# Top-k attention and a feed-forward block: the first pair of rows in two groups, weight shifts spread over four steps, and the second block's statistics one step earlier

## The chip, the cores and the metric

The kernel runs on one core of a Trainium2 chip. A core has five engines that each work through their own list of instructions in order: TensorE (PE in the profile; its weight loads are listed as PEld), VectorE (DVE), ScalarE (ACT), GpSimd (POOL) and SyncE (SP), which here only issues DMAs. An engine that needs another's result waits on a semaphore. The metric is the device time of one execution in microseconds, as the median of several runs.

## The reference

Two parts follow each other. The first is attention that keeps, for every query, the 32 largest scores; the second is layer normalisation, a feed-forward pair of matrices and a residual. All is float32, except that `w_ch1` and `w_ch2` are given as float64.

```python
# q, k, v: (8 batches, 8 heads, 576 rows, 64)
scores = scale * q @ k^T                                  # 576 x 576 for each batch and head
kth = np.partition(scores, -32)[..., -32:-31]
scores = np.where(scores >= kth, scores, -1e9)
attn = exp(scores - max); attn = attn / (sum(attn) + 1e-9)
x = (attn @ v)  as (8, 576, 512)                          # heads side by side
xn = (x - mean) / sqrt(var + 1e-6) * g_ln                 # over 512
out = x + max(xn @ w_ch1, 0) @ w_ch2                      # 512 -> 2048 -> 512
```

## The kernel before, in words

**Units, jobs, groups.** Queries are taken 128 rows at a time: four tiles of 128 and a rest of 64 per batch. A *job* is one batch, two heads side by side (`hp` from 0 to 3) and a list of such row tiles; a *unit* is one row tile of a job, for both heads. There are 160 units, and the first eight (`EARLY`) are the row tiles 0 and 1 of batch 0 for the four pairs of heads. Each job has one *group* (`Group`): its units share one transposed tile `pt`, one product with the values and one set of denominators. `pt` has a single buffer.

**Steps.** The loop `for n in range(END)` (L1266) writes out one step per unit. In step n, VectorE selects for unit n while the other engines work for its neighbours; every engine gets its instructions in the order in which this loop writes them, and nothing is reordered later. What a step does, by engine:

- PE: the scores of unit n+2 (`scores`, L434), the transposes of the weights of an earlier unit (`turn`, L602), the product with the values when a group is complete (`values`, L665 and L673) and its transposes (`place`, L710). Between these, `fill` (L269) puts pieces of the feed-forward blocks, which wait in the list `todo`.
- ACT: copies the scores from PSUM (`take_scores`, L415), scales the thresholds (`prepare`, L491 and L492), makes the mask (`mask`, L528), the exponentials (`weigh`, L539), and copies what PE transposed (L614, L642, L683). `put` (L687) scales a result into `x`.
- DVE: eight rounds on 288 columns. At the end of step n-1, `halve` splits unit n into the larger and the smaller of each two columns (L457 maximum, L458 minimum). Then `select(u, 0)` to `select(u, 3)`: MAX8 (L479, L471) finds eight largest, MATCH_REPLACE8 (L465) takes them out. `select(u, 3)` stands at the end of the step.
- POOL: subtracts the scores from the mask (L531) and writes a check (`watch`, L498).

**Weights.** The float64 weights are turned into float32 on the chip, in 32 *pieces* of 128 x 512 (class `Piece`): 0 to 15 of `w_ch1`, 16 to 31 of `w_ch2`. `fetch` (L148, SP) loads both 32-bit words; `split` has ACT take the high word's size (L164) and the low word (L166), and POOL clamp the size (L165) and the sign (L169); `shift` (L172, DVE) joins size and sign; `join` (L178, POOL) adds the low word's part and marks the piece ready. Which piece is treated in which step stands in `batches`, and in which place of the step in `weights(n, phase)` (L205): phase 0 near the step's start, phase 1 after `select(u, 1)`, phase 2 just ahead of `select(u, 3)`, phase 3 after `halve`. Pieces 0 to 3 (`batches[-1]`) are fetched and split ahead of step 0; their four shifts stand at the end of step 0 after `halve`, and their joins one in each of the steps 0 to 3. Steps 1 to 8 take one piece each (split in phase 0, shifted in phase 2, joined in phase 3 of the next step). From step `LATE` = 9 on there are two pieces a step (fetched in phase 0, split in phase 2, shifted and joined in phase 1 of the next step), the last two in step 18.

**Blocks.** Two row tiles of 128 rows are one feed-forward block. When the last pair of heads has been placed, `arrived` notes the rows, and `Block.stats` (L738 statistics, L739 their sum) makes mean and variance and takes the mean off: in the first block on DVE (L741), in all others on POOL (L744, L747). `Block.centred` says when the transposes of the rows may follow: at once in the first block, otherwise six calls of `fill` later (`CENTRE_AGE`). The block's own work is then `turn_x` (L776, L782), the hidden layer (L822, relu L845), the projection (L861 in the first two blocks, L982 in the others), the scaling (L797) and the residual (L790). Hidden and projecting matmuls wait until their piece of the weights is ready. `gives` holds the step at which a block joins `todo`: the first block, of units 0 to 7, in step 9 (`gives_first`), the second in step 19. The first block's last group is `quick`: its product, its placing and its reciprocal (L1290) stand at the very start of step 9, and its statistics in the middle of that step. The second block's rows are placed in step 18 and its statistics stand late in step 19, after `select(u, 2)`.

**Start.** `load(fresh[0], nc.sync, nc.scalar)` brings k and q of the first job with four DMAs each, k on SP's queue and q on ACT's (L303), in runs of 32 floats; DVE transposes them (L362) into `kT`, `qT` (256 columns) and `late_qT` (320 columns). Then SP fetches pieces 0 to 3 and loads the next job, for which the first job's input tile must be free.

Of the kernel before, what the change touches and what calls it, by code (L numbers as in the profile page):

```python
# [29 lines left out]
def compute(  # L30
# [162 lines left out]
        nc.scalar.copy(gcol[:], ps[:, 0:NC])  # L193


    LATE = NF // 2 + 1
    batches = {}
    queue = list(pieces)
    for n in range(-1, NF + 4):
        count = 4 if n < 0 else 0 if n == 0 else 1 if n < LATE else 2  # L200
        batches[n], queue = queue[:count], queue[count:]
    batches = {n: x for n, x in batches.items() if x}
    assert not queue
# [1 line left out]
    def weights(n, phase):  # L205

        now, before = batches.get(n, []), batches.get(n - 1, [])
        if phase == 0:
            coming = batches.get(n + 1, [])
            for x in (coming if 0 <= n < LATE - 1 else now if n >= LATE else []):  # L210
                x.fetch()
            for x in now if 0 < n < LATE else []:
                x.split()
        elif phase == 1:
            for x in before if n > LATE else []:
                x.shift()
                x.join()
        elif phase == 2:
            for x in now if n >= LATE else []:
                x.split()  # L220
            for x in now if 0 < n < LATE else []:
                x.shift()
        else:
            for x in before if 0 < n <= LATE else []:
                x.join()

    todo = []
# [63 lines left out]
    def load(job, first, second, later=False):  # L291

        job.ins = {}
        raw = ldpool.tile([P, 2, S], FP32, tag="raw", name="kqin")
        if job.whole:
            load_rows(job, raw, first, second)
            return
        for s, (name, src, queue) in enumerate((("k", k, first), ("q", q, second))):
            t = raw[:, s]

            def part(i, t=t, src=src, queue=queue):
                head, d0 = 2 * job.hp + i * 32 // D, i * 32 % D
                queue.dma_start(  # L303
                    t[i * 32 : (i + 1) * 32, :].rearrange("b (n a) -> b n a", a=32),
                    src[job.b, head, :, d0 : d0 + 32].rearrange("(n b) a -> b n a", b=32),
                )

            for i in range(P // 32):
                if later:
                    age = (4 * len(job.ins) + i) // 2  # L310
                    loads.add(lambda i=i, part=part: part(i), -age)
                else:
                    part(i)
            job.ins[name] = t
# [407 lines left out]
    class Block:  # L722
# [9 lines left out]
        def stats(self, i):  # L732
            x = self.x[i]
            if self.mv is None:
                self.mv = small.tile([P, 2, 2], FP32, tag="mv", name="mv")
                self.rstd = small.tile([P, 2], FP32, tag="rstd", name="rstd")
            st = brief_small.tile([P, 6], FP32, tag="st", name="st")
            nc.vector.bn_stats(out=st[:], in_=x)  # L738
            nc.vector.bn_aggr(out=self.mv[:, i, :], in_=st[:])  # L739
            if now[0] <= gives_first:  # L740
                nc.vector.tensor_scalar_sub(x, x, self.mv[:, i, 0:1])  # L741
            else:
                less = brief_small.tile([P, 1], FP32, tag="less", name="less")
                nc.gpsimd.tensor_scalar(  # L744
                    less[:], self.mv[:, i, 0:1], -1.0, 0.0, ALU.mult, ALU.add
                )
                nc.gpsimd.tensor_scalar(x, x, 1.0, less[:], ALU.mult, ALU.add)  # L747
            self.step[i] = tick[0]

        def centred(self, i):  # L750
            return i in self.step and (
                now[0] <= gives_first or tick[0] - self.step[i] >= CENTRE_AGE
            )

        def inverse(self):
# [324 lines left out]
    order += [(6, rows[0] + rest), (7, rows[0] + rest), (6, rows[1]), (7, rows[1])]  # L1080
    assert B == 8
    jobs = [Job(b, hp, [qts]) for b, qts in order for hp in range(NHP)]
    units = []
    for j in jobs:
        j.groups = [Group(j, qts) for qts in j.groups]
# [29 lines left out]

    for j, after_j in zip(jobs, jobs[1:] + [None]):
        waits = after_j is not None and units[after_j.first].moved
        j.groups[0].lag = 2 if j.last < EARLY else 4 if waits else 3

    full = slice(0, P)  # L1120
    gives = {}
# [9 lines left out]
    for j in jobs:  # L1131
        if j.hp == NHP - 1:
# [3 lines left out]
            dsts = [[(out[b, t[1] * P : (t[1] + 1) * P, :], full)] for t in tiles]  # L1136
            if jobs.index(j) == NHP - 1:
                step -= 1
                j.groups[0].quick = True
            if tiles:  # L1140
                add_block(step, tiles, dsts)
            if J in j.groups[0].qts and b % 4 == 3:
# [103 lines left out]
        blk.x[i] = x  # L1246
        rows_of.setdefault(n + 1, []).append((blk, i))

    gives_first = min(gives)
    load(fresh[0], nc.sync, nc.scalar)  # L1250

    nc.scalar.copy(gcol[:], half[:])
# [13 lines left out]
    for n in range(END):  # L1266
# [89 lines left out]
            scores(units[2])  # L1356
            take_scores(units[2])
        for x in (u if n < EARLY else None, mk if n > EARLY else None):
            if x and x is units[x.job.last]:
                load_values(x.job)  # L1360
                ends_due[n + 1] = x.job
        fill()
# [33 lines left out]
            select(u, 3)  # L1396
        if nxt:
            halve(nxt)
        if n == 0:
            for x in batches[-1]:  # L1400
                x.shift()
        weights(n, 3)
        for x in batches[-1][n : n + 1]:
            x.join()
        if g and not quick and g.job.hp == NHP - 1:
            for qt in g.qts:
                if qt < J:
                    arrived(n, (g.job.b, qt), xs[g.job.b, qt])
        if late and late.job.hp == NHP - 1:
            r = late.job.b // 2  # L1410
            if r % 2:
# [61 lines left out]
```

## Time and profile before

| | us |
|---|---|
| median of 3 runs | 1550.89 (1550.7 to 1552.42) |
| the profiled execution | 1550.43 |
| its span | 1548.6 |
| PE busy in the span | 1463.6 (95%) |
| DVE busy | 1362.0 (88%) |
| ACT busy | 1076.3 (70%) |
| POOL busy | 953.4 (62%) |

A line of the timeline gives the start and the time in us, the engine, the source line, the operation, the tile written and those read with their shapes, and `x` with the number of like instructions in a row, whose time is then that of the whole row. In square brackets stands how long the engine had been idle before it and what ended that. An instruction's time runs until its result is there, so two that follow each other overlap by some 0.1 us; the distance between two starts says what one of them costs its engine. SPq and ACTq are the queues on which these engines issue DMAs.

### The profile page before, as it was taken

How to read it: one execution, taken by the hardware profiler on the slowest of the kernel's cores; microseconds unless marked ns; L12 is line 12 of the kernel's file. 1: busy time of each engine (PE TensorE's matmuls, PEld its weight loads, DVE VectorE, ACT ScalarE, POOL GpSimd, SP SyncE). 2: the span in 40 equal slices, each digit the busy share in tenths (PEclk: the TensorE clock that was granted, in tenths of full speed). 3: DMA queues.
4: the chain of work that ended last, by engine and by line, in shares of the span. 5: the costliest groups of instructions: out<-in, count | busy, mean ns of one | idle time of the engine just before them, and what ended most of it. 6: DMA issues, size and time to landing. Idle time of an engine off the chain costs nothing. (4 is left out here: it accounts for less than half of the span.)

```text
span 1548.6 us, 27247 instructions
## 1 busy us (share of the span) xinstructions
PE 1463.6 (95%) x8046; PEld 1106.8 (71%) x8046; DVE 1362.0 (88%) x3873; ACT 1076.3 (70%) x3085; POOL 953.4 (62%) x1302
## 2 busy tenths in 40 slices
PE   4679989999999899999999999999999999999997
PEld 3456457576777677777777777777777777788886
DVE  7999999999899998999979999999999999867000
ACT  6978878776777678767777776867677776464421
POOL 5769978556484656666646556565656575737514
PEclk9789999999999999999999999999999999999998
DMA  7534533576648773686735686576676666454511
GB/s 196 150 97 131 154 80 106 141 179 196 177 136 211 188 204 110 192 201 164 219 105 157 170 224 184 157 186 174 189 188 184 181 177 189 133 166 120 142 36 50
DMA packets 374775, 245.61 MB, mean 159 GB/s; under 512 B 255956, under 2 KB 343512, under 8 KB 374616
## 3 DMA queue, kind: packets, MB, share of 16 engines
q1 hardware_dynamic: 371048, 243.17, 57.7%
q8 instruction: 67, 1.10, 0.3%
q10 hardware_dynamic: 3568, 0.59, 0.3%
q14 instruction: 92, 0.75, 0.2%
HBM read 166.14 MB, written 77.53 MB: 157 GB/s over the span
## 5 line engine op out<-in xcount | busy, mean ns | idle before, releaser
L531 POOL TENSOR_TENSOR e<-e,sc 128x576 f32<-128x576 f32 x288 | 416.6, 1465 | 455.0 <-ACT e L528 406.2
L822 PE MATMUL hps<-xT,w 128*128 128x256 f32 x2304 | 543.6, 385 | 0.5 <-ACT xT L782 0.5
L822 PEld LDWEIGHTS hps<-xT,w 128*128 128x128 f32 x2304 | 423.7, 191 | 80.3 <-issue 27.0
L479 DVE MAX8 m<-hi 128x8 f32<-128x296 f32 (+1 forms) x1152 | 472.1, 445 | 1.2
L465 DVE MATCH_REPLACE8 hi<-m,hi 128x288 f32<-128x288 f32 (+1 forms) x864 | 377.6, 442 | 0.0
L982 PE MATMUL ops<-w,h 128*128 128x256 f32 x1280 | 307.2, 385 | 0.0
L982 PEld LDWEIGHTS ops<-w,h 128*128 128x128 f32 x1280 | 235.1, 191 | 43.1 <-issue 14.3
L415 ACT COPY sc<-scps 128x288 f32<-128x288 f32 x576 | 188.4, 402 | 86.2 <-POOL e L531 63.6
L539 ACT ACTIVATE e<-e,m 128x576 f32<-128x576 f32 x288 | 225.1, 785 | 9.5 <-POOL e L531 7.3
L528 ACT ACTIVATE e<-sc,m 128x576 f32<-128x576 f32 x288 | 209.3, 768 | 0.0
L845 ACT ACTIVATE h<-hps 128x512 f32<-128x512 f32 x144 | 86.6, 602 | 105.3 <-PE hps L822 104.3
L573 DVE STREAM_TRANSPOSE sc<-e 128x1152 f32<-128x1152 f32 x87 | 119.0, 1367 | 45.1 <-ACT e L539 39.1
L665 PE MATMUL av<-pt,vb 128*64 128x256 f32 (+2 forms) x1280 | 143.9, 366 | 6.9 <-DMA pt<-turned 2.2
L458 DVE TENSOR_TENSOR lo<-sc 128x576 f32<-128x576 f32 (+1 forms) x160 | 135.1, 844 | 0.0
L457 DVE TENSOR_TENSOR hi<-sc 128x576 f32<-128x576 f32 (+1 forms) x160 | 122.2, 763 | 3.0 <-ACT sc L415 3.0
L665 PEld LDWEIGHTS av<-pt,vb 128*64 128x64 f32 x1280 | 79.4, 137 | 62.3 <-issue 17.4
L434 PE MATMUL scps<-kT,late_qT 64*128 64x288 f32 (+3 forms) x832 | 121.4, 410 | 0.6 <-ACT x L687 0.4
L982 PE MATMUL ops<-wt,s 128*128 128x256 f32 x512 | 119.7, 382 | 0.0
L471 DVE MAX8 hi<-lo 128x8 f32<-128x288 f32 x288 | 117.7, 444 | 0.0
L602 PE MATMUL tp<-ident,e 128*128 128x128 f32 x456 | 74.7, 292 | 37.6 <-ACT e L539 26.1
L434 PEld LDWEIGHTS scps<-kT,late_qT 64*128 64x128 f32 (+1 forms) x832 | 69.7, 168 | 51.7 <-issue 20.9
L982 PEld LDWEIGHTS ops<-wt,s 128*128 128x128 f32 x512 | 94.6, 190 | 16.6 <-issue 3.7
(108 smaller groups left out, 1778.3 us busy)
## 6 DMA issues: line engine op xcount, KB each, us to landing
turned<-sc SPq DMA_DIRECT2D x87, 576.0 KB, 4.4
pt<-turned SPq DMA_DIRECT2D x348, 144.0 KB, 3.1
w<-forms SPq DMA_DIRECT2D x128, 256.0 KB, 4.6
vb<-in_v_dram SPq DMA_DIRECT2D x80, 288.0 KB, 4.3
raw<-in_moe_w_ch_dram SPq DMA_DIRECT2D x32, 512.0 KB, 4.7
kT<-kept SPq DMA_DIRECT2D x48, 288.0 KB, 3.6
kept<-kT SPq DMA_DIRECT2D x32, 288.0 KB, 3.5
kqin<-in_k_dram SPq DMA_DIRECT2D x116, 72.0 KB, 2.6
```

What stands on the lines that cost most here:

```text
L415: nc.scalar.copy(u.sc[:, t, s * HALF : (s + 1) * HALF], u.made[s][t][:, 0:HALF])
L434: nc.tensor.matmul(ps[i * R : i * R + ql, o : o + width], qT[r, q0 : q0 + ql], kT[r, k0 : k0 + width], start=True, stop=True,)
L457: nc.vector.tensor_tensor(hi, a, b, ALU.max)
L458: nc.vector.tensor_tensor(lo, a, b, ALU.min)
L465: nc.vector.match_replace(x, m[:, t, :], x, LOWEST)
L479: nc.vector.max(m[:, t, :], u.hi[:, t, r0 : r0 + width])
L528: nc.scalar.activation(u.e[:, t], u.sc[:, t], AF.Relu, bias=u.edge[:, t : t + 1], scale=-STEEP)
L531: nc.gpsimd.tensor_tensor(u.e[:, t], u.e[:, t], u.sc[:, t], ALU.subtract)
L539: nc.scalar.activation(u.e[:, t], u.e[:, t], AF.Exp, bias=u.bias[:, t : t + 1], scale=-scale, accum_out=g.den[:, col : col + 1],)
L665: nc.tensor.matmul(av[h * D : (h + 1) * D, 0 : g.nq], vb[:, h * (J + 1) + c, :], heads_of(g, h, 0, g.nq // 32)[:, :, c], start=(c == 0), s ...
L822: nc.tensor.matmul(ps[0][:, side * N : (side + 1) * N], w1[:, c, f * P : (f + 1) * P], self.xT[:, c, 0:N], start=(c == 0), stop=(c == NC - 1),
L982: nc.tensor.matmul(bank[name][:, 0:Q], a(j), rhs, start=first and j == 0, stop=(j == G - 1), skip_group_check=not first,)
```

## The change

Four places change.

1. `LATE` becomes 8, and step 0 gets a piece of its own (piece 4, fetched in phase 0 and split in phase 2 of step 0, shifted in phase 2 and joined in phase 3 of step 1). Every later piece moves one place ahead: steps 1 to 8 take pieces 5 to 12, step 8 already fetches in phase 0 and splits in phase 2, from step 9 on there are two a step, and step 18 has one. Of pieces 0 to 3, one is shifted in phase 2 of each of the steps 0 to 3, ahead of `select(u, 3)`, instead of all four at the end of step 0; the joins stay in phase 3 of these steps. Step 1 thereby shifts pieces 1, 4 and 5, steps 2 and 3 two pieces each.
2. The first job's q comes in two halves: columns 0 to 255 on ACT's queue as before, columns 256 to 575 with four more DMAs on SP's queue, behind k and ahead of the weights.
3. The job of units 6 and 7 has two groups of one row tile each. Unit 6's product with the values is made, placed and divided at the start of step 8, its statistics in that step after `select(u, 2)`; unit 7's as before at the start of step 9.
4. The second block's statistics stand at the end of step 18, after `halve`, and its mean is taken off on DVE (L741's form) like the first block's; its transposes may follow at once.

```diff
--- before.py
+++ after.py
@@ -193,11 +193,11 @@
         nc.scalar.copy(gcol[:], ps[:, 0:NC])
 
 
-    LATE = NF // 2 + 1
+    LATE = NF // 2
     batches = {}
     queue = list(pieces)
     for n in range(-1, NF + 4):
-        count = 4 if n < 0 else 0 if n == 0 else 1 if n < LATE else 2
+        count = 4 if n < 0 else 1 if n <= LATE else 2
         batches[n], queue = queue[:count], queue[count:]
     batches = {n: x for n, x in batches.items() if x}
     assert not queue
@@ -205,23 +205,26 @@
     def weights(n, phase):
 
         now, before = batches.get(n, []), batches.get(n - 1, [])
+        late, first = n >= LATE, n == 0
         if phase == 0:
             coming = batches.get(n + 1, [])
-            for x in (coming if 0 <= n < LATE - 1 else now if n >= LATE else []):
+            for x in now if late else now + coming if first else coming if n < LATE - 1 else []:
                 x.fetch()
-            for x in now if 0 < n < LATE else []:
+            for x in [] if late or first else now:
                 x.split()
         elif phase == 1:
             for x in before if n > LATE else []:
                 x.shift()
                 x.join()
         elif phase == 2:
-            for x in now if n >= LATE else []:
+            for x in now if late or first else []:
                 x.split()
-            for x in now if 0 < n < LATE else []:
+            for x in batches[-1][n : n + 1] + (before if n == 1 else []):
+                x.shift()
+            for x in [] if late or first else now:
                 x.shift()
         else:
-            for x in before if 0 < n <= LATE else []:
+            for x in batches[-1][n : n + 1] + (before if 0 < n <= LATE else []):
                 x.join()
 
     todo = []
@@ -298,13 +301,19 @@
         for s, (name, src, queue) in enumerate((("k", k, first), ("q", q, second))):
             t = raw[:, s]
 
-            def part(i, t=t, src=src, queue=queue):
+            def part(i, t=t, src=src, queue=queue, n0=0, n1=S):
                 head, d0 = 2 * job.hp + i * 32 // D, i * 32 % D
                 queue.dma_start(
-                    t[i * 32 : (i + 1) * 32, :].rearrange("b (n a) -> b n a", a=32),
-                    src[job.b, head, :, d0 : d0 + 32].rearrange("(n b) a -> b n a", b=32),
-                )
-
+                    t[i * 32 : (i + 1) * 32, n0:n1].rearrange("b (n a) -> b n a", a=32),
+                    src[job.b, head, n0:n1, d0 : d0 + 32].rearrange("(n b) a -> b n a", b=32),
+                )
+
+            if job is fresh[0] and name == "q":
+                for n0, n1, queue in ((0, 2 * P, second), (2 * P, S, first)):
+                    for i in range(P // 32):
+                        part(i, queue=queue, n0=n0, n1=n1)
+                job.ins[name] = t
+                continue
             for i in range(P // 32):
                 if later:
                     age = (4 * len(job.ins) + i) // 2
@@ -737,7 +746,7 @@
             st = brief_small.tile([P, 6], FP32, tag="st", name="st")
             nc.vector.bn_stats(out=st[:], in_=x)
             nc.vector.bn_aggr(out=self.mv[:, i, :], in_=st[:])
-            if now[0] <= gives_first:
+            if self.soon():
                 nc.vector.tensor_scalar_sub(x, x, self.mv[:, i, 0:1])
             else:
                 less = brief_small.tile([P, 1], FP32, tag="less", name="less")
@@ -747,9 +756,12 @@
                 nc.gpsimd.tensor_scalar(x, x, 1.0, less[:], ALU.mult, ALU.add)
             self.step[i] = tick[0]
 
+        def soon(self):
+            return blocks.index(self) < PLAIN
+
         def centred(self, i):
             return i in self.step and (
-                now[0] <= gives_first or tick[0] - self.step[i] >= CENTRE_AGE
+                self.soon() or tick[0] - self.step[i] >= CENTRE_AGE
             )
 
         def inverse(self):
@@ -1080,6 +1092,7 @@
     order += [(6, rows[0] + rest), (7, rows[0] + rest), (6, rows[1]), (7, rows[1])]
     assert B == 8
     jobs = [Job(b, hp, [qts]) for b, qts in order for hp in range(NHP)]
+    jobs[NHP - 1].groups = [[qt] for qt in rows[0]]
     units = []
     for j in jobs:
         j.groups = [Group(j, qts) for qts in j.groups]
@@ -1115,7 +1128,8 @@
 
     for j, after_j in zip(jobs, jobs[1:] + [None]):
         waits = after_j is not None and units[after_j.first].moved
-        j.groups[0].lag = 2 if j.last < EARLY else 4 if waits else 3
+        for g in j.groups:
+            g.lag = 2 if j.last < EARLY else 4 if waits else 3
 
     full = slice(0, P)
     gives = {}
@@ -1136,7 +1150,8 @@
             dsts = [[(out[b, t[1] * P : (t[1] + 1) * P, :], full)] for t in tiles]
             if jobs.index(j) == NHP - 1:
                 step -= 1
-                j.groups[0].quick = True
+                for g in j.groups:
+                    g.quick = True
             if tiles:
                 add_block(step, tiles, dsts)
             if J in j.groups[0].qts and b % 4 == 3:
@@ -1246,7 +1261,7 @@
         blk.x[i] = x
         rows_of.setdefault(n + 1, []).append((blk, i))
 
-    gives_first = min(gives)
+    gives_first, soon_after = sorted(gives)[:PLAIN]
     load(fresh[0], nc.sync, nc.scalar)
 
     nc.scalar.copy(gcol[:], half[:])
@@ -1356,7 +1371,7 @@
             scores(units[2])
             take_scores(units[2])
         for x in (u if n < EARLY else None, mk if n > EARLY else None):
-            if x and x is units[x.job.last]:
+            if x and x is units[x.job.last + 1 - len(x.job.groups)]:
                 load_values(x.job)
                 ends_due[n + 1] = x.job
         fill()
@@ -1396,16 +1411,14 @@
             select(u, 3)
         if nxt:
             halve(nxt)
-        if n == 0:
-            for x in batches[-1]:
-                x.shift()
         weights(n, 3)
-        for x in batches[-1][n : n + 1]:
-            x.join()
         if g and not quick and g.job.hp == NHP - 1:
             for qt in g.qts:
                 if qt < J:
                     arrived(n, (g.job.b, qt), xs[g.job.b, qt])
+            if n + 1 == soon_after:
+                for blk, i in rows_of.pop(n + 1):
+                    blk.stats(i)
         if late and late.job.hp == NHP - 1:
             r = late.job.b // 2
             if r % 2:
```

## The prediction

> **What bounds the kernel now.** I read the page's busy shares first, then the busy time by stretches, then VectorE's waits, and last the timeline of single engines in the first 215 us, where every instruction that the change touches lies.
>
> ```profile
> 11.20:400.00 388.80, 339.22 (x1711) 228.77 (x1710) 386.99 (x1089) 311.88 (x855) 275.42 (x290) 0.93 0.52 144
> 400.00:900.00 500.00, 490.60 (x2991) 380.85 (x2988) 468.67 (x1349) 367.27 (x1102) 301.52 (x438) 1.00 0.64 171
> 900.00:1300.00 400.00, 393.33 (x2140) 297.03 (x2140) 398.00 (x1153) 292.67 (x855) 246.25 (x361) 1.00 0.68 183
> 1300.00:1460.00 160.00, 160.00 (x826) 131.11 (x825) 105.15 (x278) 84.27 (x227) 98.32 (x147) 1.00 0.55 151
> ```
> ```profile
> DVE wt L172 <- POOL sign L169: 1.2, 1, 1.2
> ```
>
> Columns of the first view: length, then PE, PEld, DVE, ACT, POOL. From 11.2 to 400 us VectorE (DVE) is busy 386.99 of 388.80 us and TensorE (PE) 339.22; DVE's waits there after its first operation are the one line of 1.2 us. So DVE paces the stretch in which the change lies. From 400 to 900 PE is the fuller one, from 900 to 1300 DVE again, and from 1300 on PE is busy throughout with what is left of the blocks. The steps are written out in a fixed order, so time that DVE gains or loses before 220 us moves all that follows, unless the 31 us that DVE idles between 400 and 900 take it in (a rival below).
>
> But "busy" hides a wait. DVE operations with two tensors as input (shift L172, maximum L457, minimum L458) and POOL's operations take turns:
>
> ```profile
> 119.41 3.24 POOL L531 TENSOR_TENSOR e<-e,sc 128x576 f32<-128x576 f32 x2
> ...
> 122.76 3.03 POOL L178 TENSOR_TENSOR w<-wt 128x512 uint32<-128x512 uint32 x2
> ```
> ```profile
> 119.49 1.89 DVE L172 SCALAR_TENSOR_TENSOR wt<-wt,sign 128x512 uint32<-128x512 uint32 x1 [1.25 <-POOL sign L169]
> ...
> 123.66 1.00 DVE L457 TENSOR_TENSOR hi<-sc 128x576 f32<-128x576 f32 x1
> 124.58 1.83 DVE L458 TENSOR_TENSOR lo<-sc 128x576 f32<-128x576 f32 x1
> 126.33 0.81 DVE L479 MAX8 m<-hi 128x8 f32<-128x288 f32 x2
> ```
>
> Two joins (L178) run from 122.76. L457 comes at 123.66, is through at 124.58, and L458 needs until 126.33: each waited for the join that was running, and POOL took its turn between them. At 119.49 a shift released by POOL's sign (L169) comes just behind POOL's next operation and takes 1.89 us.
>
> **The change, part by part.** *Weight shifts.* The DVE order of the first steps now:
>
> ```profile
> 18.70 1.02 DVE L457 TENSOR_TENSOR hi<-sc 128x576 f32<-128x576 f32 x1
> 19.65 1.19 DVE L458 TENSOR_TENSOR lo<-sc 128x576 f32<-128x576 f32 x1
> 20.76 4.77 DVE L172 SCALAR_TENSOR_TENSOR size<-size,sign 128x512 uint32<-128x512 uint32 x4
> 25.45 0.81 DVE L479 MAX8 m<-hi 128x8 f32<-128x288 f32 x2
> ...
> 30.93 0.67 DVE L172 SCALAR_TENSOR_TENSOR size<-size,sign 128x512 uint32<-128x512 uint32 x1
> 31.53 0.82 DVE L479 MAX8 m<-hi 128x8 f32<-128x296 f32 x2
> 32.27 0.73 DVE L457 TENSOR_TENSOR hi<-sc 128x576 f32<-128x576 f32 x1
> 32.93 0.74 DVE L458 TENSOR_TENSOR lo<-sc 128x576 f32<-128x576 f32 x1
> 33.60 0.81 DVE L479 MAX8 m<-hi 128x8 f32<-128x288 f32 x2
> ...
> 51.68 0.45 DVE L479 MAX8 m<-hi 128x8 f32<-128x288 f32 x1
> ```
>
> Undisturbed starts follow each other by 0.60 (shift), 0.74 (MAX8 pair), 0.66 (L457) and 0.67 us (L458); step 1, from 25.45 to 33.60, is 8.15 us, 5.48 of it ahead of its shift. Step 0's tail (18.70 to 25.45) takes 6.75 us where 0.66 + 0.67 + 4 x 0.60 = 3.73 would do: 3.0 us of turns lost to POOL. Steps 2 and 3 (33.60 to 51.68) take 18.08 for 16.30, of which 0.1 is a reciprocal: 1.7 lost. In all 4.7 us, which the spreading could save. But it moves three other things. Piece 4's split goes into step 0, on ACT and POOL ahead of unit 0's mask; step 1 shifts three pieces (1, 4, 5); and the joins of pieces 1 to 3, whose shifts were long done, now follow their own shift, beside L457 and L458 of the same step.
>
> ```profile
> 17.77 0.66 POOL L169 TENSOR_SCALAR sign<-raw 128x512 f32<-128x512 f32 x1
> ...
> 27.04 0.61 POOL L165 TENSOR_SCALAR size<-size 128x512 f32<-128x512 f32 x1
> 27.74 0.66 POOL L169 TENSOR_SCALAR sign<-raw 128x512 f32<-128x512 f32 x1
> 28.35 1.28 POOL L178 TENSOR_TENSOR w<-size,wt 128x512 uint32<-128x512 uint32 x1
> 33.48 2.85 POOL L531 TENSOR_TENSOR e<-e,sc 128x576 f32<-128x576 f32 x2 [3.85 <-ACT e L528]
> ```
> ```profile
> 21.15 1.00 ACT L415 COPY sc<-scps 128x288 f32<-128x288 f32 x3 [0.56 <-PE scps L434]
> ...
> 22.28 1.44 ACT L528 ACTIVATE e<-sc,m 128x576 f32<-128x576 f32 x2
> ```
>
> With all 0.7 us earlier (next part): shift 0 comes at 17.26, waits for an L169 until 17.73; L457 waits 0.6 for the next; step 0 ends at 20.95 instead of 25.45. Step 1 reaches its shifts at 26.4. POOL: ACT's L164 of piece 4 ends about 22.15; L165 and L169 to 23.5, join 0 (1.28) to 24.8, the two L531 (1.4 each) to 26.2 and 27.6. Shift 1 waits for 27.6, shift 4 ends at 29.0; then POOL does L165 and L169 of piece 5, to 30.3, for which shift 5 waits; join 1 is ahead of it as at 119.49, so it ends at 32.2. L457 meets join 4 and starts at 33.5; the step ends at 34.8 instead of 33.60, with four shifts done, not five. The early gain is spent on waiting for POOL. Steps 2 and 3 each hold one shift more (0.60). Their joins start when the second shift lets go (1.2 us after the first began) and end at 2.48; L457 would come at 1.94 and waits 0.54, the second join slips in ahead of L458 for 1.28: 1.8 lost, so 10.55 us each. Step 3 ends at 34.8 + 21.1 + 0.1 = 56.0 instead of 51.68: +4.3, start included. One shift is then ahead of the old order and is given back in step 19: **+3.7**. Bounds: nothing lost to turns any more would be -4.3 (minus 4.7, plus 1.1 in step 0, minus 0.7); one more join's length lost gives +5. I take the turns as the rows at 119 and 123 us show them.
>
> The Trainium skill, page "SBUF — State Buffer", section "Who interferes with whom", says that a DVE instruction with two SBUF inputs and a GpSimd one that reads SBUF exclude each other for the whole instruction, whichever issued first; the rows at 123 us agree.
>
> *Start.* q comes in two column halves, the second on SP's queue behind k.
>
> ```profile
> q1 hardware_dynamic: 2367, 0.31, 45.7%
> q10 hardware_dynamic: 2214, 0.28, 41.2%
> ```
> ```profile
> 6.62 0.78 DVE L362 STREAM_TRANSPOSE kT<-kqin 128x576 f32<-128x576 f32 x1 [6.62 <-DMA kqin<-in_k_dram]
> ```
>
> Those are the packets of SP's queue (k) and ACT's (q) up to 5.2 us: they share the engines evenly and nearly all 4608 are through. 320 of q's 576 columns, 1280 packets, now come behind k: at 4581 packets in some 3.4 us that is 0.9 us less ahead of the first transpose. Bounds 0 and -0.9; I take **-0.7** (contained in the +3.7), since k's last issue still limits. Four more issues on SP (0.5 us each) put the weights' fetch 2 us later, and late_qT's transpose waits for them; DVE has no other work until 11.14, and ACT needs the first weights at 13.41: hidden. If not, each us is a us.
>
> *First block's last pair.* One reciprocal more (**+0.1**); one tile's statistics go from step 9 to 8 and a shift from 8 to 9: even. Twenty short matmuls instead of ten long ones fall where PE is idle. ACT places tile 0 ahead of unit 7's mask, which comes some 3 us later; POOL's wait covers it:
>
> ```profile
> 96.70 2.94 POOL L531 TENSOR_TENSOR e<-e,sc 128x576 f32<-128x576 f32 x2 [6.74 <-ACT e L528]
> 97.42 0.97 DVE L741 TENSOR_SCALAR x<-x,mv 128x512 f32<-128x512 f32 x1
> 98.31 0.68 DVE L738 BATCH_NORM_STATS2 st<-x 128x6 f32<-128x512 f32 x1
> ...
> 99.24 0.69 DVE L741 TENSOR_SCALAR x<-x,mv 128x512 f32<-128x512 f32 x1
> ...
> 99.85 0.82 DVE L479 MAX8 m<-hi 128x8 f32<-128x296 f32 x2
> ```
>
> If the cover is gone, tile 1's x is late for DVE: up to +1.5.
>
> *Second block's statistics.* The subtraction moves from POOL (L744, L747) to DVE: twice 0.61 to 0.89 us, **+1.5**. A turn lost to L747 goes: L458 took 1.09, not 0.67, **-0.4**. The rows it needs are placed long before step 18 ends at 203:
>
> ```profile
> 212.81 1.17 DVE L458 TENSOR_TENSOR lo<-sc 128x576 f32<-128x576 f32 x1
> 213.90 0.81 DVE L479 MAX8 m<-hi 128x8 f32<-128x288 f32 x2
> ```
> ```profile
> 197.63 0.93 ACT L687 ACTIVATE x<-xo,den 128x64 f32<-128x64 f32 x4 [1.80 <-DVE den L1349]
> ```
>
> *PE.* Half of the second weight's pieces come a step earlier and the second block's rows some slots earlier; by the two orders PE is four matmuls ahead at step 20, one at the end: 0.2 to 0.9 us, taken as **-0.3**.
>
> Sum: 3.7 + 0.1 + 1.5 - 0.4 - 0.3 = +4.6. The profiled execution took 1550.43 us (span 1548.6), which becomes 1555.0; the median of the runs stands 0.46 above it: 1555.5.
>
> **The rivals.** *Faster:* POOL keeps pace. If piece 5's sign is there when DVE reaches shift 5 (about 29 us) and the joins find gaps, the 4.7 us of lost turns go: -4.3 + 0.1 + 1.1 - 0.3 = -3.4, 1547.5. For it: MAX8 and MATCH_REPLACE8 are not held up by POOL, so there are gaps. Against: the chain on POOL above, with no slack. It decides at whether shift 5 waits more than about 1 us. *Absorbed:* the delay reaches 400 us, and there DVE idles anyway: then only the rest counts, about +1, 1552. Against: PE's own idle time before 400 follows DVE, and 900 to 1300 is DVE's again. Half the turns lost gives the same time. *Dearer subtraction:* the two moved subtractions run beside POOL's L531 of step 18; waiting for one each (1.4) would add 2.5: 1558. Row 97.42 against 99.24 shows 0.28 only. The same page of the Trainium skill names tensor_scalar among the operations that can take both ports and so be locked out; by that rule this rival would hold.
>
> **How the numbers follow.** As forecast 0.50, dearer 0.08, absorbed or halved 0.29, faster 0.13. What a measurement can tell is 0.2%, 3.1 us: forecast and dearer are mostly above 1554.0, so slower 0.55; same 0.32; faster 0.13 with its tail. The forecast's own range is 1552.5 to 1559 (lost turns +1 to +5, subtraction 1.2 to 3). The range reaches down to 1549.5 for the absorbed case, up to 1559.5.
>
> **What would show it.** Right: L172 at the end of step 1 with a wait for L169 of 1 us or more; L457 and L458 of steps 2 and 3 above 1 us; step 4 beginning near 56 us; two more L741 near 205 us; DVE still without gaps to 400. Wrong: step 4 beginning before 52 us, a first transpose not before 6.5, or the difference at 220 us not found again at the end.

## The result and the profile after

The changed kernel takes 1554.82 us (median of 16 runs, 1551.22 to 1556.99); the kernel before, beside it on the same chip, 1550.89 (16 runs, 1547.94 to 1552.55). The ratio is 1.003, with a 95% interval of 1.0023 to 1.0037: by the medians 3.9 us slower, where 4.6 were forecast. The profiled execution took 1553.96 us (span 1552.2), 3.53 more than the one before. In the changed kernel the later lines have moved: L457, L458, L479 and L531 are now L466, L467, L488 and L540; L738 and L741 are L747 and L750; L362 is L371.

Busy time by stretches, changed kernel (start:end, length, then PE, PEld, DVE, ACT, POOL, granted clock, DMA share, GB/s):

```profile
10.50:400.00 389.50, 338.48 (x1715) 228.48 (x1713) 384.32 (x1082) 310.07 (x850) 274.97 (x285) 0.92 0.52 142
```

The bounds are where they were: DVE is busy 384.32 of 389.50 us up to 400, and PE is busy for all of the 160 us from 1300 to 1460. Of the loss these sums show only that DVE now idles 5.2 us up to 400, against 1.8 before: its waits, of which more below. An operation that waits for its turn counts as busy, so what the turns cost is seen only in the order of the first steps. DVE in the changed kernel, from the timeline:

```profile
17.30 0.68 DVE L172 SCALAR_TENSOR_TENSOR size<-size,sign 128x512 uint32<-128x512 uint32 x1
...
18.64 0.74 DVE L466 TENSOR_TENSOR hi<-sc 128x576 f32<-128x576 f32 x1
19.30 0.75 DVE L467 TENSOR_TENSOR lo<-sc 128x576 f32<-128x576 f32 x1
19.97 0.81 DVE L488 MAX8 m<-hi 128x8 f32<-128x288 f32 x2
...
25.45 3.42 DVE L172 SCALAR_TENSOR_TENSOR size<-size,sign 128x512 uint32<-128x512 uint32 x2
31.76 1.75 DVE L172 SCALAR_TENSOR_TENSOR size<-size,sign 128x512 uint32<-128x512 uint32 x1 [2.89 <-POOL sign L169]
33.43 0.83 DVE L488 MAX8 m<-hi 128x8 f32<-128x296 f32 x2
34.18 1.07 DVE L466 TENSOR_TENSOR hi<-sc 128x576 f32<-128x576 f32 x1
...
35.84 0.81 DVE L488 MAX8 m<-hi 128x8 f32<-128x288 f32 x2
...
41.32 1.27 DVE L172 SCALAR_TENSOR_TENSOR size<-size,sign 128x512 uint32<-128x512 uint32 x2
...
43.27 1.07 DVE L466 TENSOR_TENSOR hi<-sc 128x576 f32<-128x576 f32 x1
44.27 1.83 DVE L467 TENSOR_TENSOR lo<-sc 128x576 f32<-128x576 f32 x1
46.02 0.81 DVE L488 MAX8 m<-hi 128x8 f32<-128x288 f32 x2
...
56.24 0.81 DVE L488 MAX8 m<-hi 128x8 f32<-128x288 f32 x2
```

Step 1 begins at 19.97 instead of 25.45, so step 0 brings a gain of 5.48 us. Step 2 begins at 35.84 instead of 33.60: step 1 has spent the gain and 2.24 us more. Step 1 lasts 15.87 us, where its work undisturbed and two more shifts would take 8.15 + 2 x 0.60 = 9.35. The missing 6.5 us are 2.2 in the two shifts at 25.45 (3.42 for 1.20), 2.89 of waiting for piece 5's sign, 1.1 in the shift at 31.76 and 0.3 in L466. Steps 2 and 3 lose 1.4 us each, nearly all in L466 and L467. Step 4 begins at 56.24, against 51.68 before.

What POOL does meanwhile, in the changed kernel's timeline:

```profile
18.58 1.95 POOL L165 TENSOR_SCALAR size<-size 128x512 f32<-128x512 f32 x1
...
23.91 0.61 POOL L165 TENSOR_SCALAR size<-size 128x512 f32<-128x512 f32 x1 [1.24 <-ACT size L164]
...
25.23 1.27 POOL L178 TENSOR_TENSOR w<-size,wt 128x512 uint32<-128x512 uint32 x1
26.46 3.67 POOL L540 TENSOR_TENSOR e<-e,sc 128x576 f32<-128x576 f32 x2
...
31.06 0.67 POOL L169 TENSOR_SCALAR sign<-raw 128x512 f32<-128x512 f32 x1
31.68 2.95 POOL L178 TENSOR_TENSOR w<-size,wt 128x512 uint32<-128x512 uint32 x2
...
42.08 3.40 POOL L178 TENSOR_TENSOR w<-size,wt 128x512 uint32<-128x512 uint32 x2 [1.93 <-DVE size L172]
```

The row at 31.06 is the one for which DVE stands still from 28.87 to 31.76. Ahead of it on POOL's list are piece 4's clamps, join 0, the two L540 and piece 5's own L165. The joins (L178) start the moment the sign or the shift is there, and L172, L466 and L467 of DVE fall on them.

### The profile page after: what moved, and what is told of

Read it like the earlier page. It is cut to its first block, busy times and chain, and to the rows that moved or that the text cites. A ratio compares the mean times of both kernels' runs of the same rounds, so it can differ in the third digit from the quotient of the medians.

```text
span 1552.2 us, 27296 instructions
## 1 busy us (share of the span) xinstructions
PE 1466.9 (95%) x8066; PEld 1108.2 (71%) x8066; DVE 1362.4 (88%) x3876; ACT 1077.4 (69%) x3087; POOL 952.7 (61%) x1298
## 5 line engine op out<-in xcount | busy, mean ns | idle before, releaser
L540 POOL TENSOR_TENSOR e<-e,sc 128x576 f32<-128x576 f32 x288 | 420.9, 1480 | 453.8 <-ACT e L537 411.5
L488 DVE MAX8 m<-hi 128x8 f32<-128x296 f32 (+1 forms) x1152 | 471.9, 445 | 1.2
L674 PE MATMUL av<-pt,vb 128*64 128x256 f32 (+3 forms) x1296 | 147.7, 370 | 7.6 <-DMA pt<-turned 4.3
L467 DVE TENSOR_TENSOR lo<-sc 128x576 f32<-128x576 f32 (+1 forms) x160 | 132.8, 830 | 0.0
L466 DVE TENSOR_TENSOR hi<-sc 128x576 f32<-128x576 f32 (+1 forms) x160 | 124.0, 775 | 3.0 <-ACT sc L424 3.0
```

The source lines that it names most:

```text
L466: nc.vector.tensor_tensor(hi, a, b, ALU.max)
L467: nc.vector.tensor_tensor(lo, a, b, ALU.min)
L488: nc.vector.max(m[:, t, :], u.hi[:, t, r0 : r0 + width])
L540: nc.gpsimd.tensor_tensor(u.e[:, t], u.e[:, t], u.sc[:, t], ALU.subtract)
L674: nc.tensor.matmul(av[h * D : (h + 1) * D, 0 : g.nq], vb[:, h * (J + 1) + c, :], heads_of(g, h, 0, g.nq // 32)[:, :, c], start=(c == 0), s ...
```

## The experiments

Theory: the new place of the shifts costs 4 to 5 us in steps 1 to 3, by the wait for piece 5's sign and by joins that run beside DVE's two-input operations, and this reaches the end. Against it stand three others: that the delay is taken in by DVE's later idle time and the time comes from the other parts; that the subtraction on DVE is the dear one; and that the wait is due not to the order of work but to the weights or the gain vector arriving late behind q. Offsets below are differences of the start of DVE's L457 (of the same unit) from the profile before.

### The four parts, each alone

Shifts alone:

```diff
-    LATE = NF // 2 + 1
+    LATE = NF // 2
-        count = 4 if n < 0 else 0 if n == 0 else 1 if n < LATE else 2
+        count = 4 if n < 0 else 1 if n <= LATE else 2
+            for x in batches[-1][n : n + 1] + (before if n == 1 else []):
+                x.shift()
...
-        if n == 0:
-            for x in batches[-1]:
-                x.shift()
```

> Only the weight schedule of the change (one more piece in step 0, shifts of pieces 0 to 3 one in each of the steps 0 to 3); load, groups and statistics as before. Theory A (turns with POOL): the first transposes start at 6.6 us as before, step 0 ends some 4 to 5 us earlier than before, and by the start of step 4 (51.68 us before) all of it is lost and more: it starts between 55 and 57.5 us, with L458 of steps 2 and 3 near 1.8 us; time +2 to +5 us, most of the change's +3.9. Theory B (the divided load of q makes the loss, because SP's queue is longer): step 4 starts within 1.5 us of 51.68 and the time is within 1.5 us of before.

Halves of q alone:

```diff
+            if job is fresh[0] and name == "q":
+                for n0, n1, queue in ((0, 2 * P, second), (2 * P, S, first)):
+                    for i in range(P // 32):
+                        part(i, queue=queue, n0=n0, n1=n1)
```

> Only q's load in two halves. Theory A: the first transposes start 0.5 to 0.9 us earlier; the gain vector and the second job's rows come later (in the changed kernel ACT waited 1.54 us for the gain's transpose and POOL's first operation moved from 14.21 to 15.29 us), but DVE's list does not wait for them before step 1; step 4 starts 0.7 us earlier than before or at most 1 us later; time -1 to +1 us. Theory B: step 4 starts 2 us or more later, time +2 to +4 us.

Groups alone:

```diff
+    jobs[NHP - 1].groups = [[qt] for qt in rows[0]]
-            if x and x is units[x.job.last]:
+            if x and x is units[x.job.last + 1 - len(x.job.groups)]:
```

> Only the two groups of units 6 and 7. Theory A: up to step 8 nothing moves; step 9's halving for unit 10 (102.20 us before) starts within 1 us of before; time within 1 us of before. Theory B says nothing else here. If the delayed mask of unit 7 costs DVE, DVE shows a wait for x ahead of L738 in step 9 and the time rises by up to 1.5 us.

Statistics alone:

```diff
-            if now[0] <= gives_first:
+            if self.soon():
+            if n + 1 == soon_after:
+                for blk, i in rows_of.pop(n + 1):
+                    blk.stats(i)
```

> Only the second block's statistics, one step earlier and with the mean taken off on DVE. Up to step 18 nothing moves. Prediction's sum: two subtractions of 0.6 to 0.9 us more on DVE, less 0.4 us, +1.1 us at the halving of unit 22 (227.74 us before), time +0.5 to +1.5 us. Dearer subtraction: two subtractions above 1.5 us each and +3 us or more. If the earlier rows let PE work ahead, -1 us or better at the end.

| kernel | ratio to before (95%) | median, before beside it |
|---|---|---|
| shifts alone | 1.0024 (1.0014 to 1.0033) | 1555.62, 1551.3 |
| halves alone | 0.9985 (0.9975 to 0.9995) | 1549.92, 1551.3 |
| groups alone | 1.0018 (1.0009 to 1.0027) | 1554.03, 1551.3 |
| statistics alone | 1.001 (1.0001 to 1.0018) | 1552.7, 1551.3 |

The sum of the four is +0.37%, the whole change +0.30% (0.23 to 0.37). The shifts alone show the same pattern as the whole, in the timeline of DVE:

```profile
30.70 1.75 DVE L172 SCALAR_TENSOR_TENSOR size<-size,sign 128x512 uint32<-128x512 uint32 x1 [1.25 <-POOL sign L169]
...
43.20 1.82 DVE L461 TENSOR_TENSOR lo<-sc 128x576 f32<-128x576 f32 x1
...
55.17 0.81 DVE L482 MAX8 m<-hi 128x8 f32<-128x288 f32 x2
```

So the wait is there with q in one piece too; it is 1.25 us then, and 2.89 in the whole change. The halves bring the first transposes 0.55 us earlier and a gain of 0.15%, 2.3 us, more than these 0.55 and than the 1 us at most that was expected; where the rest comes from the profiles do not tell. The statistics alone move unit 21 by 1.04 us (1.78 less 0.74 at unit 19). The groups alone change nothing up to unit 8 (offset -0.74, won in step 0), but at unit 10 DVE is 1.3 us later (0.58). It is lost in step 8:

```profile
91.42 1.75 DVE L172 SCALAR_TENSOR_TENSOR size<-size,sign 128x512 uint32<-128x512 uint32 x1 [0.57 <-POOL sign L169]
```

Unit 7's mask comes later there, and POOL's operations behind it come later too (its L531 begins at 86.94, against 84.29 before), so the shift of that step, which took 0.68 us before, waits for its sign and then for a join. The runs are 0.18% slower, 2.8 us; for the rest of that no row of the first 110 us accounts.

### The kernel before once more

No edit. It tells how far two executions of one kernel agree.

> The kernel before once more, nothing changed: how far one profiled execution differs from another. Expected: DVE's steps up to 400 us within 1 us of the first profile, and between 400 and 900 us up to 1.5 us apart, since all four single parts were 1 to 4 us later there than that profile whatever they changed.

The ratio is 1.0006 (0.9997 to 1.0014). The profiles agree within 0.1 us up to unit 9 and within 0.6 up to unit 15; at unit 16 they part by 1.65 us, and at unit 79 they are 3 us apart. A single profile therefore says what happens in the first 150 us; later only the timed ratios do, and what all profiles of one kind have and the others lack.

### Where the wait comes from

No piece in step 0, so that POOL does not clamp piece 4 ahead of unit 0's mask:

```diff
-    LATE = NF // 2
+    LATE = NF // 2 + 1
-        count = 4 if n < 0 else 1 if n <= LATE else 2
+        count = 4 if n < 0 else 0 if n == 0 else 1 if n < LATE else 2
```

> The changed kernel with the pieces in the steps of the kernel before (no piece in step 0), while the shifts of pieces 0 to 3 stay spread. Theory A (POOL's chain in step 1, because piece 4 is split ahead of unit 0's mask): the wait of shift 5 for its sign (2.89 us) goes or falls below 1 us, and step 4, 56.24 us in the changed kernel, begins between 51 and 53; time 2 to 4 us below the changed kernel. Theory B (the joins beside the halving cost, the early piece does not): step 4 begins after 54.5 us and the time stays within 1.5 us of the changed kernel.

The gain vector's DMA ahead of the weights on SP's queue:

```diff
     load(fresh[0], nc.sync, nc.scalar)
+    nc.sync.dma_start(grow[:], g_ln.rearrange("(c p) -> c p", p=P))
...
-    nc.sync.dma_start(grow[:], g_ln.rearrange("(c p) -> c p", p=P))
```

> The changed kernel with the gain vector fetched ahead of the first weights instead of behind them. If the late gain vector holds ACT up in front of the first split (1.54 us of waiting in the changed kernel), that wait goes, POOL's first operation moves from 15.29 to about 14, the wait of shift 5 falls from 2.89 us to between 1.2 and 2, and step 4 begins about 1 us earlier than 56.24; time -0.5 to -1.5 us against the changed kernel. If the late second job (its rows land behind the weights) sets it instead, POOL's first operation moves but step 4 stays within 0.3 us.

Without the early piece, from DVE's timeline:

```profile
28.87 1.75 DVE L172 SCALAR_TENSOR_TENSOR size<-size,sign 128x512 uint32<-128x512 uint32 x1 [1.52 <-POOL sign L169]
...
41.05 1.82 DVE L467 TENSOR_TENSOR lo<-sc 128x576 f32<-128x576 f32 x1
...
53.01 0.81 DVE L488 MAX8 m<-hi 128x8 f32<-128x288 f32 x2
```

With the gain vector first:

```profile
29.99 1.75 DVE L172 SCALAR_TENSOR_TENSOR size<-size,sign 128x512 uint32<-128x512 uint32 x1 [1.24 <-POOL sign L169]
...
54.47 0.81 DVE L488 MAX8 m<-hi 128x8 f32<-128x288 f32 x2
```

Step 4 comes 3.2 us earlier without the early piece (0.6 of which is one shift less until then), and 1.8 us earlier with the gain vector first. So both the order of POOL's list and the late vector delay step 4. The length of the wait is a weaker sign. It was expected to fall below 1 us without the early piece and did not, and the kernel without the groups (below), which begins as the changed kernel does, waits only 1.53 us and still begins step 4 at 55.79. The times show less: 1.002 (1.0011 to 1.0029; median 1553.95, before 1551.28) and 1.0023 (1.0012 to 1.0034; 1555.89). Against the whole change's 1.003 that is 1.6 and 1.1 us, with intervals that overlap, so how much of an earlier step 4 comes back at the end is not settled by these two.

### Where the turns come from

As the kernel without the early piece, with the joins of pieces 1 to 3 one step later:

```diff
-            for x in batches[-1][n : n + 1] + (before if 0 < n <= LATE else []):
+            own = batches[-1][:1] if n == 0 else batches[-1][n - 1 : n] if n > 1 else []
+            for x in own + (before if 0 < n <= LATE else []):
                 x.join()
```

> The changed kernel without the early piece (as in the run before it), and with the joins of pieces 1, 2 and 3 one step later, so that they follow POOL's sign instead of their own shift. Theory A (POOL and DVE take turns, so a join costs DVE where it meets a two-input operation): the minimum (L467) of steps 2 and 3 falls from 1.82 to 0.75 us, the last shift of step 1 from 1.75 to 0.7, but the pair of shifts in steps 2 and 3 rises from 1.28 to between 2.5 and 3.5 us, because the joins now meet these; step 4 begins within 1.2 us of 53.0. Rival (the joins beside the halving are a loss of their own): the minimum falls, the shifts stay at 1.28, and step 4 begins 3 us earlier, below 50.5; time 2 to 3 us below that kernel.

DVE's timeline:

```profile
28.62 0.69 DVE L172 SCALAR_TENSOR_TENSOR size<-size,sign 128x512 uint32<-128x512 uint32 x1 [1.51 <-POOL sign L169]
...
36.77 2.72 DVE L172 SCALAR_TENSOR_TENSOR size<-size,sign 128x512 uint32<-128x512 uint32 x2
...
41.17 0.75 DVE L468 TENSOR_TENSOR lo<-sc 128x576 f32<-128x576 f32 x1
...
51.95 0.81 DVE L489 MAX8 m<-hi 128x8 f32<-128x288 f32 x2
```

The shift behind the wait now takes 0.69 us instead of 1.75, since no join starts with it, and L468 takes 0.75 instead of 1.82. But the pairs of shifts take 2.72 and 2.58 us instead of 1.28: the joins, released by POOL's own list, meet them there. Step 4 comes 1.06 us earlier, which is the turn saved in step 1; the 2.8 us that steps 2 and 3 lose are lost again, at the shifts. The lost turn moves to whichever two-input operation of DVE the join meets. The ratio is 1.0014 (1.0003 to 1.0026; 1554.26, before 1552.15).

### The change without its groups, and without its shifts

Without groups:

```diff
-    jobs[NHP - 1].groups = [[qt] for qt in rows[0]]
```

> The changed kernel with the job of units 6 and 7 in one group again. If the parts add up (alone: +0.24%, -0.15%, +0.18%, +0.10%), the ratio to the kernel before is 1.002 (0.19% left); if the two groups cost nothing and their +0.18% alone was chance, it stays at 1.003 as with the whole change. Step 9's halving (unit 10) is within 1 us of the changed kernel.

Without shifts (halves, groups and statistics kept):

```diff
-    LATE = NF // 2
+    LATE = NF // 2 + 1
...
+        if n == 0:
+            for x in batches[-1]:
+                x.shift()
```

> The changed kernel with the weights' schedule of the kernel before. Theory A: the loss up to step 4 goes; step 4 begins 0.5 to 1 us earlier than 51.68, as with the halves alone; ratio 1.0005 to 1.0015 (the sum of the other three parts alone, 0.13%). Rival (the parts act together, the load of q being what delays POOL): step 4 begins after 53 us and the ratio stays above 1.002.

Without the groups: 1.0021 (1.001 to 1.0033; 1555.92, before 1552.15), step 4 at 55.79. Without the shifts: 1.0 (0.9989 to 1.0012; 1553.28, before 1552.15), step 4 at 51.20. Taking out the new places of the weights (part 1, the early piece included) removes the whole loss, though the other three alone add up to 0.13%; taking the groups out leaves a ratio whose interval overlaps that of the whole change.

### A version that beats both

The halves of q and the gain vector ahead of the weights, on the kernel before:

```diff
+            if job is fresh[0] and name == "q":
+                for n0, n1, queue in ((0, 2 * P, second), (2 * P, S, first)):
...
     load(fresh[0], nc.sync, nc.scalar)
+    nc.sync.dma_start(grow[:], g_ln.rearrange("(c p) -> c p", p=P))
```

> The kernel before with q's load in two halves and the gain vector ahead of the weights; nothing else of the change. Step 4 begins 0.7 to 2 us earlier than 51.68; time 1 to 4 us below the kernel before, a version faster than both.

The same kernel once more:

> The kernel before with q's load in two halves and the gain vector ahead of the weights, measured a second time because its first interval (0.998 to 0.9997) ends close to 1. If the 2 us that DVE is ahead at step 4 reach the end, the ratio is again 0.998 to 0.9995 and step 4 begins within 0.5 us of 49.7; if the first result was chance, the interval holds 1.0 or more.

The two sets give 0.9989 (0.998 to 0.9997; 1548.6, before 1551.28) and 0.9983 (0.9974 to 0.9992; 1549.18, before 1551.91): 1.7 and 2.6 us faster than before. DVE's tail of step 0, in the profile of the first set and in that of the second:

```profile
20.01 3.56 DVE L172 SCALAR_TENSOR_TENSOR size<-size,sign 128x512 uint32<-128x512 uint32 x4
```
```profile
20.10 4.77 DVE L172 SCALAR_TENSOR_TENSOR size<-size,sign 128x512 uint32<-128x512 uint32 x4
```

One turn more or less (3.56 against 4.77 for the same four shifts) is a matter of the single execution, and step 4 begins at 49.72 in one and 51.06 in the other. The second expectation on that start, within 0.5 us of the first, was therefore missed, while the ratio came as expected. The halves alone had 0.9985, so what the gain vector adds cannot be told from nothing.

## Why the prediction was right

**Direction, size and range.** 1554.82 lies 0.7 us below the forecast of 1555.5 and inside 1549.5 to 1559.5. The cause is the predicted one as far as step 4: the gain of step 0 is spent on waiting for POOL, and the whole loss goes with part 1 of the change (1.0 without it). On the way from step 4 to the end the forecast held in size, but in part by luck (see "Absorbed" and "DVE without gaps").

**The shifts, step by step.** The start of step 4 was forecast at 56.0 and is 56.24, which is luck, since errors cancel: step 0 ended at 19.97, not 20.95 (1.0 less); step 1 took 15.87, not 13.85 (2.0 more); steps 2 and 3 took 20.4 together, not 21.2 (0.8 less). In step 0 the sum had the shift and L466 wait for clamps. Neither did (0.68 us at 17.30, 0.74 at 18.64); POOL waited instead, its L165 at 18.58 taking 1.95 us where it takes 0.61 undisturbed, while L466 and L467 both went ahead of it. In step 1 the wait for piece 5's sign was 2.89 us, not 1.3. In steps 2 and 3 L466 and L467 lost turns as forecast, 1.4 us a step in place of 1.8.

**The step that failed** is "ACT needs the first weights at 13.41: hidden". The weights were not late (with the gain vector first, ACT takes them at 12.87), but the gain vector behind them was. In the changed kernel PE's and ACT's timelines have

```profile
14.21 0.23 PE L192 MATMUL tp<-ident,grow 4*128 4x4 f32 x1 [2.69 <-DMA grow<-in_moe_g_ln_dram]
```
```profile
14.47 0.16 ACT L193 COPY columns<-tp 128x4 f32<-128x4 f32 x1 [1.54 <-PE tp L192]
14.53 0.67 ACT L164 ACTIVATE size<-raw 128x512 f32<-128x512 f32 x1
```

where ACT's first L164 came at 13.41 before. The prediction let everything run 0.7 us earlier; DVE did, but ACT came to the weights 1.1 us later, and POOL with it: piece 4's clamp began at 23.91, some 1.8 us after the sum's 22.15. With the gain vector first, step 1 begins at 20.83 (the sum has 20.95), the wait for piece 5's sign is 1.24 us (the sum has 1.3) and step 4 begins at 54.47: there the sum is borne out at the start and is 1.5 us too long by step 4. The kernel without the groups has the vector late as well (ACT's first L164 at 14.09). It ended step 0 at 20.99, waited 1.53 us and began step 4 at 55.79. So the late vector costs 1.3 to 1.8 us by step 4. The turns won in step 0 of the changed kernel's profile, and the longer wait behind them, belong to that one execution.

**The start.** First transpose 0.66 us earlier (forecast 0.7):

```profile
5.96 0.78 DVE L371 STREAM_TRANSPOSE kT<-kqin 128x576 f32<-128x576 f32 x1 [5.96 <-DMA kqin<-in_q_dram]
```

**The groups.** Forecast +0.1. In the whole change DVE's offset goes from 4.56 at unit 8 to 4.65 at unit 10, and without the groups from 4.09 to 3.84, so they cost 0.1 to 0.3 us there. Alone they cost 1.3: the old order shifts a piece in step 8 that POOL clamps in that step, behind unit 7's mask, and the wait of POOL that the prediction took for cover does not cover this shift. The new order has no shift in step 8. In the timed runs the groups alone cost 0.18% (2.8 us), beyond the bound of +1.5 us that the prediction set for a cover that is gone; in the whole change, leaving them out saves 0.09%, which the intervals do not separate from nothing. Whether they have a cost of their own at the end stays open.

**The statistics.** Forecast +1.1 (1.5 for two subtractions, 0.4 back from L458). DVE before, then the changed kernel's DVE and POOL at that place:

```profile
209.82 0.68 DVE L738 BATCH_NORM_STATS2 st<-x 128x6 f32<-128x512 f32 x1
...
210.64 0.66 DVE L738 BATCH_NORM_STATS2 st<-x 128x6 f32<-128x512 f32 x1
```
```profile
205.53 0.68 DVE L747 BATCH_NORM_STATS2 st<-x 128x6 f32<-128x512 f32 x1
...
206.47 0.69 DVE L750 TENSOR_SCALAR x<-x,mv 128x512 f32<-128x512 f32 x1
207.08 0.68 DVE L747 BATCH_NORM_STATS2 st<-x 128x6 f32<-128x512 f32 x1
...
208.01 0.69 DVE L750 TENSOR_SCALAR x<-x,mv 128x512 f32<-128x512 f32 x1
...
216.10 0.75 DVE L467 TENSOR_TENSOR lo<-sc 128x576 f32<-128x576 f32 x1
```
```profile
204.97 3.44 POOL L540 TENSOR_TENSOR e<-e,sc 128x576 f32<-128x576 f32 x2
```

From the first tile's statistics to the second's it is 1.55 us now (205.53 to 207.08) and was 0.82 before (209.82 to 210.64): 0.73 more for a tile, 1.5 for two, as forecast. L467 of the next step took 0.75, against 1.17 before. The statistics alone gave 1.04, so this term came true. The rival of the dearer subtraction does not, here: the first runs while POOL has the two L540, the second begins before they end, and both take 0.69 us, where

```profile
95.44 0.49 DVE L750 TENSOR_SCALAR x<-x,mv 128x512 f32<-128x512 f32 x1
...
103.38 1.19 DVE L750 TENSOR_SCALAR x<-x,mv 128x512 f32<-128x512 f32 x1
```

show one with POOL all but idle (0.49) and one that began 0.5 us into an L540 (1.19). In the second execution of the kernel before there is one that took what the rival had feared:

```profile
97.51 1.55 DVE L741 TENSOR_SCALAR x<-x,mv 128x512 f32<-128x512 f32 x1
```

It began 1.48 us into a pair of L531 that took 2.76, so just behind the start of the second. A subtraction does wait for POOL, then, for the rest of the operation that runs (0.2, 0.2, 0.7 and 1.1 us here), and how much that is depends on when it comes. The prediction's 0.28 for row 97.42 against 99.24 was too little, because the 0.69 of row 99.24 had itself waited 0.2. The Trainium skill, page "SBUF — State Buffer", section "Who interferes with whom", counts tensor_scalar among those that can be locked out; these rows agree with the rule.

**Absorbed.** The prediction's test was whether the difference at 220 us is found again at the end. In the profiles it is 2.86 us at unit 22 and 3.53 at the end, in the timed runs 3.9, and the kernel without the shifts is level with the one before. So a loss of the forecast's size does reach the end, and it goes with part 1, though the 1.8 to 3.2 us by which two experiments began step 4 earlier were not clearly returned. That it is the loss of steps 1 to 3 that arrives is not shown. The offset falls from 4.56 at unit 8 to 1.42 at unit 24 and is back at 3.27 at unit 27, behind a new wait (next paragraph but one); and the kernel before, run again without an edit, is itself 2.38 us off at unit 22. One thing was not foreseen: between units 12 and 15 the changed kernel makes up 2.4 us (offset 4.85 to 2.48). One of three pairs of shifts there, before and after, from DVE's timelines:

```profile
142.81 2.60 DVE L172 SCALAR_TENSOR_TENSOR wt<-wt,sign 128x512 uint32<-128x512 uint32 x2
```
```profile
146.82 1.32 DVE L172 SCALAR_TENSOR_TENSOR wt<-wt,sign 128x512 uint32<-128x512 uint32 x2
```

The three take 8.89 us before and 6.81 after. Turns are lost and won again by where POOL's operations fall.

**PE.** The prediction counted -0.3 us because PE would be four matmuls ahead at step 20. It was ahead, but the rows show no gain from it. PE in that step, before and after:

```profile
212.27 3.70 PE L861 MATMUL ops<-w,h 128*128 128x512 f32 x8
```
```profile
214.68 1.98 PE L873 MATMUL ops<-w,h 128*128 128x512 f32 x4
...
217.57 1.09 PE L788 MATMUL tp<-ident,x 128*128 128x128 f32 x8 [0.91 <-ACT sc L424]
219.82 4.15 PE L834 MATMUL hps<-xT,w 128*128 128x256 f32 x18 [1.16 <-ACT xT L794]
```

With four projecting matmuls left for this place instead of eight, PE came early to the next block's transposes and stood idle 0.91 and 1.16 us; before, it idled 0.50 there. Its scores, 2.4 us later than before at the unit ahead (209.74, against 207.32), are 4.2 us later at the next (227.70, against 223.50).

**DVE without gaps.** This sign did not come true. Besides the two waits in the first 35 us there is one more before 400:

```profile
271.16 1.38 DVE L582 STREAM_TRANSPOSE sc<-e 128x1152 f32<-128x1152 f32 x1 [1.74 <-ACT e L548]
```

DVE waits for ACT's exponential, and that stands in ACT's list behind a copy that waits for PE's transposes. The wait is in all four kernels that have the early piece (whole change 1.74 us, shifts alone 5.77, gain vector first 5.12, without groups 1.74), each of which also has four projecting matmuls in the place above. In none of the other ten profiles does this transpose wait before 400 us. That PE's new order makes the wait is read from these rows; no run changes it alone.

## What to carry to other kernels

When work is moved to even out one engine, write out the list of the engine that feeds it: here VectorE's gain of 5.5 us was gone one step later, where GpSimd had a new piece of work ahead of the one that VectorE waits for. A small DMA at the end of a queue (the gain vector, behind the new halves and the weights) can be the one that holds an engine; look for its reader, not only for the large transfers. An engine that is ahead has gained nothing if its next work is not there yet. And a cost hidden in turns does not show in busy shares: compare each row's duration with the shortest of its kind.

## What the runs showed of the hardware

- Operations of DVE with two inputs and POOL's operations hold each other up, mostly in turns. When DVE starts behind the POOL operation that released it, POOL's next goes first: the shift took 1.75 us at 28.87 with a join next on POOL's list, and 0.69 at 28.62 without one. The turns are not strict: POOL's L165 at 18.58 let two operations of DVE pass and took 1.95 us instead of 0.61.
- POOL loses to DVE as well: the two L540 at 204.97, which met L467, took 3.44 us, those at 92.61 with DVE's two-input work elsewhere 2.77.
- Identical programs part by a whole turn: 3.56 against 4.77 us for the same four shifts, a jump of 1.65 us at unit 16 between two executions of the kernel before.
- With q in halves SP issued the last k rows of the second job at 15.25 us instead of 9.77; the profile has it waiting 3.9 us there for DMAs of q's rows. With the gain vector first it was 11.14, and a wait of 3.9 us for q's rows stood one issue later. What held it was not settled.
